# A hand-written issue order remade: batches 1 and 2 read the state in two places, and unread TensorE products stand in four groups instead of three

## The chip, the cores and the metric

The kernel runs on one core of a Trainium2 chip. The metric is the device time of one execution in microseconds (us), lower is better. Five engines work side by side, each through its own instructions in program order: PE (TensorE, the matrix engine; its loads of the stationary operand are shown apart as PEld), DVE (VectorE), ACT (ScalarE), POOL (GpSimd) and SP, which here only starts transfers (DMA) between the main memory and the core. An engine waits for another through semaphores. Matrix products land in PSUM, which holds eight banks of 128 x 512 words here, and have to be copied or used from there by DVE or ACT before the bank is free again.

## The reference

Eight batches, eight heads, 512 tokens and 32 state rows per head, width 64. Tokens attend to the state rows, the state rows attend to the tokens, and both results, side by side along the token axis (512 + 32 = 544 rows of 512 channels for each batch), run through a block with a causal convolution as gate.

```python
scores = x @ state.T / 8;   xread = softmax(scores) @ state     # 512 tokens read the state
scores2 = state @ x.T / 8;  sread = softmax(scores2) @ x        # 32 state rows read the tokens
h = concat([xread, sread])                                      # (8, 544, 512), heads side by side
gate = sigmoid(causal_conv(h, conv_w, 5 taps))
out = (gate * (h @ w_val)) @ w_out
```

(The reference's setup draws 576 rows for the second block's own example; here the block gets the 544 rows above.)

## The kernel before, in words

Every batch b goes through the same steps. `scores` (tile `sc`, two PSUM banks) multiplies the state by the batch's transposed tokens. For the tokens' side DVE transposes the scores in 32 x 32 blocks (`sl`), takes the maximum (`mx`), POOL subtracts and later scales, ACT takes the exponent (`ex`). For the state's side DVE takes the row maximum (`nb`), ACT the exponent (`e2`), PE transposes it (`exp_T`, tile `e2p`), ACT copies it out (`e2T`), and `state_read` multiplies it by the tokens: 32 products of 32 x 64 for a batch, each of two passes, so 64 matrix instructions and 64 weight loads on tile `srp`. `state_read_copy` (tile `sr`), `state_read_T` (tile `srT`) and `state_read_out` turn the result into the 32 extra rows, which a tail treats for all batches at the end. `state_val` (tile `sgv`) multiplies the state by the weights, and `read` (tile `xr`) the probabilities by the state; DVE, ACT and POOL form the convolution gate from `xr` (tiles `acc`, `last`, `sig`). `values` (tile `val`) makes the values, `gated` (tile `g`) multiplies them by the gate, `high` and `low` split `g` into a high part on ACT (`gh`) and a low part on POOL (`gl`), and `project` multiplies by the output weights with three products for each of four channel blocks (tile `op`, lines 512 to 514). ACT or DVE copies `op` to `o`, and SP stores it. Batch 0 is treated in a simpler form: its `values` products use plain four-byte data and take longer (tile `a0` by `sw0`).

Work of the start: ACT, POOL and DVE decode the weights, which lie in memory as 64-bit words (`words_part`, `words_side`, `words_sum`, `words_join`: tiles `wt`, `ws`, `wv`, `wc`), and PE spreads the convolution weights over partitions (tile `cwbp`, copied by ACT to `cwb`; tile `cwtp`, copied to `cwt`). POOL multiplies the state by `cwb` for batch 0 (`tap_state`, shown as z<-z,cwb).

`warm_up` multiplies a tile of ones by itself, `n` products of 128 x 128 in two passes each. Nothing reads the result. `WARM` gives the size of each group.

What runs when is written out by hand. All steps are numbered in the order in which the batches' code lists them; `ORDER` is a list of these numbers, and the last loop of the kernel issues them in that order, with a letter where the engine can be chosen (a is ACT, v or none is DVE, g is POOL). Each engine therefore gets its instructions in the order of this list. `SLOTS` says for each new tile which of its buffers it takes; `ps` is the list of PSUM banks.

Of the kernel before, what the change touches and what calls it, by code (L numbers as in the profile page):

```python
# [36 lines left out]
WARM = (9, 2, 14)  # L37
# [3 lines left out]
68 15 0 8 69 20 25 158 2 6 1 55 40 9 969 71 10a 35 11 74 73 12 75 970 72 30 81 13 76g 14a 82 22a 91 70 77 83 21 78 84g  # L41
267 26 89 79g 85 23 27a 86 971 18 16 92 28 3 87g 96 19a 24 17a 160 90 29 109g 80 97a 103 88 94 105a 57g 104a 171 110
95a 169 172 161 56 162 37a 58 170 163 32g 36 31 59 176 42a 38 45 122 164g 114 93 4 33 115 39 41 118 34 116 66g 177a 43
165 123 67g 106 44 117 269 166 124a 50 111g 108a 185 7 125g 107a 159 47a 271 98 60a 167g 99 119 46 178 268 280 100 126
376 48 281 594 61g 270 120a 49 52a 130 121g 272 62a 51 127 63g 188a 140 53 179a 287 128a 131 273g 134 186a 54 141 5
278 64a 146 168 288a 65g 147 279 187 135 274 129g 189 190 132a 275 133g 101 191 136 173a 148 193 276g 142 194 102a
199a 237 195 198 149 192a 200 137 196g 201 143 277 152 174g 197 153 284 205 202 154 144a 175 150a 155 207 138a 203g
219 208 156a 139 225 213a 209 151 226 282g 212 157 220 227 206a 214 238 204 221 215 285 228 294 210g 222 229a 216 378
223a 297a 217g 180 485 295a 380 181 145 286a 387 290 224g 182 389 289 388 298 183 239 184a 230g 218 379 231 291 232
240 390 299 283g 296 241a 381 211 292 233 293a 394 307 234 334 300 242g 309 328 395a 346 302 321 335 382g 310 329 301a  # L50
340 311 341 303 308a 347 336 323 383 312g 342 304 348 235a 324 243 305g 313 255 325 315a 384 330 236g 322a 256 314 244
326g 306 337 257 316 258 385g 331 245 393 332a 317 246 259a 318 333g 260 403 247a 386 377 338a 248 487 404a 339g 486
406a 396 703 489 327 249 319g 391a 498 250 405 499 251 392g 488 397a 252 349 320 407 261 253a 496 408 490 505 424a 343
# [28 lines left out]
    x="0100101000",  # L82
    xT="01001001",
    sT="01",
    e2="0001000111020202",
    e2T="0120122102101001",
    sr="00000000",
    sl="00101010",
    ah="01001100101",
    al="0110011010",  # L90
    swh="0100110010",
    swl="011001101",
    acc="0120201221022011210102101202",
    last="0110100101011010011110110101",
# [703 lines left out]
```

## Time and profile before

| | |
|---|---|
| median of three runs | 211.48 us (211.03 to 211.58) |
| the profiled execution, its own time | 212.08 us |
| its span, first to last instruction | 209.9 us |
| PE busy | 203.2 us (97%) |
| DVE, ACT, POOL busy | 159.4, 155.2, 152.5 us |

The time of an execution holds some two microseconds that lie around the span. Busy time of PE is the time in which at least one product is shown as running; products overlap, so the distance from one start to the next tells more than the length of one.

### The profile page before, as it was taken

Reading aid. Unit: us, or ns where it says so; the run is one execution under the profiler, and the core shown is the slowest. Engines: PE = TensorE matmul, PEld = TensorE weight load, DVE = VectorE, ACT = ScalarE, POOL = GpSimd, SP = SyncE. Lnnn points to the kernel's source line nnn. Section 1 sums busy time; section 2 is a strip of 40 time slices with the busy share of each in tenths; the row PEclk is TensorE's granted clock in tenths of the full one; section 3 lists DMA queues with packets and bytes.
Section 4 is the critical chain, followed back from the end, with each engine's and each line's share of the span. In section 5 each row is a group of like instructions: output and inputs, shape, how many; then the busy total and the mean of one; then the engine's idle time right before and its main releaser. Section 6 shows DMA issues by size and latency. Waiting matters only on the chain.

```text
span 209.9 us, 4603 instructions
## 1 busy us (share of the span) xinstructions
PE 203.2 (97%) x1781; PEld 147.0 (70%) x1781; DVE 159.4 (76%) x255; ACT 155.2 (74%) x325; POOL 152.5 (73%) x118
## 2 busy tenths in 40 slices
PE   7799999999999999999999999999999999999994
PEld 6654457676688567766777857577866788988883
DVE  1799999998999988998969759998895988630000
ACT  3498999977987978789755989799879964333123
POOL 2286999999979938988938596948799999473000
PEclk9999999999999999999999999999999999999998
DMA  6999689604700692048016028182011200002525
GB/s 182 417 370 425 263 248 425 284 0 153 253 0 2 187 415 100 0 101 303 0 55 250 3 62 279 25 286 103 0 52 53 101 0 3 0 0 100 186 79 188
DMA packets 9507, 31.24 MB, mean 149 GB/s; under 512 B 1146, under 2 KB 1678, under 8 KB 7566
## 3 DMA queue, kind: packets, MB, share of 16 engines
q1 hardware_dynamic: 9342, 30.43, 39.9%
q10 hardware_dynamic: 144, 0.52, 1.0%
q8 instruction: 14, 0.23, 0.4%
q14 instruction: 7, 0.06, 0.1%
HBM read 22.04 MB, written 8.91 MB: 147 GB/s over the span
## 4 chain that ended last, share of the span: by engine, by line
PE 86%; DVE 4%; issue 1%; ACT 1%; ACTq 0%
PE val L503 21%; PE op L512 13%; PE op L514 13%; PE op L513 13%; PE srp L377 4%; PE e2p L368 4%; PE xr L439 3%; PE sgv L324 3%; PE tval L580 3%; PE sc L353 3%; DVE acc L483 2%; PE xr L454 2%; PE top L513 1%; PE top L514 1%; PE top L512 1%
## 5 line engine op out<-in xcount | busy, mean ns | idle before, releaser
L483 DVE SCALAR_TENSOR_TENSOR acc<-xr,cwt,acc 128x511 f32<-128x511 f32 (+2 forms) x84 | 60.3, 741 | 6.0 <-ACT last L216 2.4
L512 PE MATMUL op<-woh,gh 128*128 128x512 f32 x124 | 50.1, 404 | 0.2 <-DVE acc L483 0.2
L514 PE MATMUL op<-woh,gl 128*128 128x512 f32 x124 | 49.1, 396 | 0.0
L513 PE MATMUL op<-wol,gh 128*128 128x512 f32 x124 | 48.9, 394 | 0.0
L221 POOL TENSOR_TENSOR gl<-g,gh 128x512 fp32r<-128x512 f32 x32 | 41.2, 1295 | 7.7 <-ACT gh L208 7.5
L221 POOL TENSOR_TENSOR acc<-acc,last 128x508 f32<-128x508 f32 x28 | 35.9, 1286 | 12.8 <-DVE acc L483 7.0
L512 PEld LDWEIGHTS op<-woh,gh 128*128 128x128 f32 x124 | 23.4, 189 | 6.3 <-issue 0.6
L514 PEld LDWEIGHTS op<-woh,gl 128*128 128x128 f32 x124 | 23.3, 188 | 5.6 <-POOL gl L221 0.3
L513 PEld LDWEIGHTS op<-wol,gh 128*128 128x128 f32 x124 | 23.3, 188 | 5.0 <-issue 0.2
L208 ACT CAST gh<-g 128x512 fp32r<-128x512 f32 x30 | 18.7, 632 | 10.1 <-DVE g L508 8.0
L208 ACT COPY o<-op 128x512 f32<-128x512 f32 (+1 forms) x33 | 18.4, 579 | 10.1 <-PE op L514 8.3
L508 DVE SCALAR_TENSOR_TENSOR g<-sig,val 128x512 f32<-128x512 f32 x32 | 21.3, 675 | 5.7 <-POOL tgl L221 1.5
L216 ACT ACTIVATE last<-xr,cwt 128x508 f32<-128x508 f32 x28 | 19.7, 708 | 6.5 <-DVE acc L483 5.0
L221 POOL TENSOR_TENSOR sl<-sl,mx 128x1024 f32<-128x1024 f32 (+1 forms) x9 | 15.6, 1729 | 7.3 <-DVE mx L410 7.2
L495 ACT ACTIVATE sig<-acc 128x512 f32<-128x512 f32 x28 | 17.9, 641 | 2.6 <-POOL acc L221 2.6
L478 ACT ACTIVATE acc<-xr,cwt 128x512 f32<-128x512 f32 x28 | 19.3, 708 | 0.7 <-PE xr L439 0.5
L221 POOL TENSOR_TENSOR al<-sl,ah 128x1024 fp32r<-128x1024 f32 x7 | 16.9, 2413 | 2.5 <-ACT ah L208 2.3
L503 PE MATMUL val<-ah,swh 128*128 128x512 f32 x56 | 17.2, 403 | 0.0
L503 PE MATMUL val<-al,swh 128*128 128x512 f32 x56 | 17.1, 395 | 0.0
L503 PE MATMUL val<-ah,swl 128*128 128x512 f32 x56 | 16.7, 397 | 0.4 <-issue 0.4
L221 POOL TENSOR_TENSOR ex<-ex,rc 128x1024 f32<-128x1024 f32 (+1 forms) x9 | 15.6, 1729 | 1.6 <-DMA z<-z_in 0.9
L332 DVE SCALAR_TENSOR_TENSOR swl<-sgv,swh 128x512 fp32r<-128x512 f32 x14 | 9.3, 676 | 5.5 <-ACT swh L216 5.5
(120 smaller groups left out, 378.3 us busy)
## 6 DMA issues: line engine op xcount, KB each, us to landing
x<-x_in SPq DMA_DIRECT2D x8, 1024.0 KB, 7.2
out<-o SPq DMA_DIRECT2D x31, 256.0 KB, 2.3
xT<-xT_in SPq DMA_DIRECT2D x7, 1024.0 KB, 10.9
vw<-w_val SPq DMA_DIRECT2D x4, 511.8 KB, 9.4
ow<-w_out SPq DMA_DIRECT2D x4, 511.8 KB, 5.2
xT<-xT_in ACTq DMA_DIRECT2D x1, 512.0 KB, 4.8
xT<-xT_in SPq DMA_DIRECT2D x1, 512.0 KB, 5.3
z<-z_in SPq DMA_DIRECT2D x2, 256.0 KB, 7.9
```

The lines of the kernel that those rows point to most:

```text
L208: nc.scalar.copy(out, in_)
L216: nc.scalar.mul(out, in_, factor)
L221: (nc.vector if e == "DVE" else nc.gpsimd).tensor_tensor(out, a, b, op=how)
L332: nc.vector.scalar_tensor_tensor(get("swl", b)[:, g], get("sgv", b, g), HALF / SCALE, get("swh", b)[:, g].bitcast(F32), op0=ALU.mult, op1= ...
L478: nc.scalar.mul(get("acc", b, pr), pt, cw[:, HALO, pr:pr + 1])
L483: nc.vector.scalar_tensor_tensor(acc[:, d:], get("xr", b, pr)[:, :S - d], cw[:, HALO - d, pr:pr + 1], acc[:, d:], op0=ALU.mult, op1=ALU.add)
L495: nc.scalar.activation(get("sig", b, pr), get("acc", b, pr), AF.Tanh, scale=0.5)
L503: nc.tensor.matmul(get("val", b, k), w[:, g, c], a[:, g], start=(term == 0 and g == 0), stop=(term == terms - 1 and g == NG - 1))
L508: nc.vector.scalar_tensor_tensor(get("g", b, k), get("sig", b, k), 1.0, get("val", b, k), op0=ALU.add, op1=ALU.mult)
L512: nc.tensor.matmul(pt, gh, woh[:, k], start=(k == 0), stop=False)
L513: nc.tensor.matmul(pt, gh, wol[:, k], start=False, stop=False)
L514: nc.tensor.matmul(pt, gl, woh[:, k], start=False, stop=(k == NPR - 1))
```

## The change

The list `ORDER` is replaced by another that holds the same steps, `SLOTS` is replaced by buffers to fit it, and `WARM` has two more entries: 9 + 2 + 7 + 7 + 1 = 26 unread products instead of 9 + 2 + 14 = 25. No function is touched.

```diff
-WARM = (9, 2, 14)
+WARM = (9, 2, 7, 7, 1)
 ORDER = """
-68 15 0 8 69 20 25 158 2 6 1 55 40 9 969 71 10a 35 11 74 73 12 75 970 72 30 81 13 76g 14a 82 22a 91 70 77 83 21 78 84g
+68 15 0 8 69 20 25 2 6 158 1 55 35 10a 969 71 9 40 11 73 74 12 75 970 72 30 82 76g 81 21 91 70 22a 83 971 13 16 77 89
...
 SLOTS = dict(
     ps=
-    "06126005634267501024315671027614305672465276124300127146753231763245041567746302041372520631672135460573642014"
+    "71207370465727576101234607561262571304137153657124001765726513404671053023431637547601543142670635104561075342"
...
```

What the lists do to each engine's instructions is seen in the built programs. Rows read: line, operation, tile written, tiles read, size, and a count of equal neighbours. The number after the tile's name is the batch.

First PE at about a quarter of the program, where batches 1 and 2 read the state. Before:

```order
L353 MATMUL sc_3_1_732<-xT_3_490,sT_0_97 32x512
L377 MATMUL srp_1_745<-x_1_430,e2T_1_0_374 32x64 x16
L377 MATMUL srp_1_745<-x_1_430,e2T_1_1_525 32x64 x16
L377 MATMUL srp_2_788<-x_2_480,e2T_2_1_555 32x64 x16
L377 MATMUL srp_2_788<-x_2_480,e2T_2_0_784 32x64 x16
L393 MATMUL srT_1_831<-ident_64,sr_1_807 128x128
L503 MATMUL val_1_3_614<-ah_1_600,swl_1_563 128x512 x2
L503 MATMUL val_1_2_841<-ah_1_600,swh_1_518 128x512 x2
```

With the change, the same batches:

```order
L503 MATMUL val_1_0_677<-ah_1_619,swl_1_565 128x512 x2
L377 MATMUL srp_1_700<-x_1_480,e2T_1_0_385 32x64 x16
L377 MATMUL srp_1_700<-x_1_480,e2T_1_1_498 32x64 x16
L324 MATMUL sgv_2_0_737<-wv_65,sT_0_97 32x512
```

```order
L393 MATMUL srT_1_770<-ident_64,sr_1_749 128x128
L503 MATMUL val_1_2_772<-ah_1_619,swh_1_521 128x512 x2
L503 MATMUL val_1_3_780<-ah_1_619,swh_1_521 128x512 x2
L503 MATMUL val_1_2_772<-al_1_626,swh_1_521 128x512 x2
L503 MATMUL val_1_2_772<-ah_1_619,swl_1_565 128x512 x2
L503 MATMUL val_1_3_780<-al_1_626,swh_1_521 128x512 x2
L503 MATMUL val_1_3_780<-ah_1_619,swl_1_565 128x512 x2
L377 MATMUL srp_2_810<-x_2_473,e2T_2_0_752 32x64 x16
L377 MATMUL srp_2_810<-x_2_473,e2T_2_1_553 32x64 x16
L439 MATMUL xr_2_0_853<-sl_2_495,z_73 64x512
```

The two reads stood back to back, 64 products or 128 matrix instructions in a row; now `sgv` and `sc` of the next batches, a transpose and twelve `val` products of 512 columns stand between them.

Then PE in the first part, where the unread products stand. Before:

```order
L353 MATMUL sc_0_1_129<-xT_0_94,sT_0_97 32x256
L271 MATMUL cwtp_162<-ident_64,cv_68 128x20
L314 MATMUL warm_2_194<-blank_78 128x128 x14
L261 MATMUL cwbp_1_209<-cv_68,sel_71 128x128
L261 MATMUL cwbp_0_211<-cv_68,sel_71 128x128 x4
L368 MATMUL e2p_0_1_221<-ident_64,e2_0_1_216 128x128 x4
L353 MATMUL sc_1_0_229<-xT_1_106,sT_0_97 32x512
```

With the change:

```order
L353 MATMUL sc_0_1_129<-xT_0_94,sT_0_97 32x256
L314 MATMUL warm_2_173<-blank_78 128x128 x7
L271 MATMUL cwtp_181<-ident_64,cv_68 128x20
L261 MATMUL cwbp_0_183<-cv_68,sel_71 128x128 x4
L261 MATMUL cwbp_1_196<-cv_68,sel_71 128x128
L314 MATMUL warm_3_214<-blank_78 128x128 x7
L368 MATMUL e2p_0_1_222<-ident_64,e2_0_1_209 128x128 x4
L314 MATMUL warm_4_231<-blank_78 128x128
L353 MATMUL sc_1_0_233<-xT_1_108,sT_0_97 32x512
```

The group of 14 is now two groups of 7 on either side of the convolution's products, and one more unread product stands behind the first transposes.

Last ACT at about an eighth of the program, where batch 0's second half of `sgv` is copied out as `sw0`. Before:

```order
L208 COPY e2T_1_0_374<-e2p_1_0_340 128x512
L417 ACTIVATE ex_75<-sl_1_320 128x32x32
L474 ACTIVATE sig_0_3_393<-xr_0_3_277 128x512
L208 CAST gh_0_1_409<-g_0_1_378 128x512
L216 ACTIVATE sw0_0_264<-sgv_0_1_1_383 128x256
L216 ACTIVATE sw0_0_264<-sgv_0_0_1_381 128x256
L287 ACTIVATE ws_o_1_432<-ow1_1_348,edge_70 128x512
L208 CAST woh_66<-wc_o_0_391 128x512
```

With the change:

```order
L417 ACTIVATE ex_75<-sl_1_323 128x32x32
L208 COPY e2T_1_0_385<-e2p_1_0_352 128x512
L208 CAST gh_0_1_423<-g_0_1_380 128x512
L279 ACTIVATE wt_o_1_437<-ow1_1_348,edge_70 128x512
L208 CAST gh_0_0_445<-g_0_0_404 128x512
L287 ACTIVATE ws_o_1_461<-ow1_1_348,edge_70 128x512
L216 ACTIVATE sw0_0_267<-sgv_0_0_1_449 128x256
L216 ACTIVATE sw0_0_267<-sgv_0_1_1_451 128x256
L208 CAST woh_66<-wc_o_0_425 128x512
```

The two copies now stand behind both decoding passes of a weight block and behind `gh` of batch 0, block 0. By `SLOTS` the next transposes of batch 1 (`e2p_1_1`) take the bank of `sgv_0_0_1`, and the next `val` products the bank of `sgv_0_1_1`, so both wait for these copies.

## Rows read from the trace of the kernel before

**Rows 1.** The page: busy time, share of the span, instructions; a DMA queue.

```profile
PE 203.2 (97%) x1781; PEld 147.0 (70%) x1781; DVE 159.4 (76%) x255; ACT 155.2 (74%) x325; POOL 152.5 (73%) x118
...
q8 instruction: 14, 0.23, 0.4%
```

**Rows 2.** Busy by stretch: stretch, length, PE, PEld, DVE, ACT, POOL, clock, DMA, GB/s.

```profile
30.00:40.00 10.00, 10.00 (x53) 6.17 (x52) 9.70 (x14) 9.75 (x20) 10.00 (x9) 1.00 0.95 394
```

**Rows 3.** PE in time at state_read of batches 1 and 2: start, length, instruction, count.

```profile
51.72 2.01 PE L377 MATMUL srp<-x,e2T 128*32 128x64 f32 x128
53.66 0.33 PE L393 MATMUL srT<-ident,sr 128*128 128x128 f32 x1
54.35 0.62 PE L503 MATMUL val<-ah,swl 128*128 128x512 f32 x2 [0.36 <-issue]
54.81 0.63 PE L503 MATMUL val<-ah,swh 128*128 128x512 f32 x2
```

**Rows 4.** PE in time, the same transpose for another batch.

```profile
92.52 0.33 PE L393 MATMUL srT<-ident,sr 128*128 128x128 f32 x1
...
93.16 0.62 PE L503 MATMUL val<-al,swh 128*128 128x512 f32 x2
```

**Rows 5.** DMA queues from 51.5 to 53.1 us: packets, MB, share.

```profile
q8 instruction: 1, 0.02, 5.6%
```

**Rows 6.** The chain that ended last, in order of time: start, us, what.

```profile
23.25 1.98 PE val L503 x4
...
27.54 1.03 PE srp L377 x64
28.57 0.59 PE e2p L368 x4
29.16 3.44 PE val L503 x8
...
33.43 0.44 PE e2p L368 x4
...
51.79 1.94 PE srp L377 x128
```

**Rows 7.** The start in time, three engines.

```profile
13.49 0.66 PE L368 MATMUL e2p<-ident,e 128*128 128x128 f32 x4 [0.41 <-ACT e L361]
13.76 1.27 DVE L304 SCALAR_TENSOR_TENSOR wv<-vw,wt_v 128x512 int32<-128x512 int32 x2
14.55 1.60 POOL L221 TENSOR_TENSOR z<-z,cwb 128x640 f32<-128x640 f32 x1
15.09 0.67 PE L340 MATMUL sgv<-wv,sT 64*32 64x256 f32 x16
16.40 4.54 PE L454 MATMUL xr<-a,z 32*64 32x512 f32 x80
```

**Rows 8.** An unread group of 14 products in time.

```profile
8.39 3.39 PE L314 MATMUL warm<-blank 128*128 128x128 f32 x28
```

**Rows 9.** PE in time at another place where it waits.

```profile
103.57 0.40 PE L514 MATMUL op<-woh,gl 128*128 128x512 f32 x1
104.14 0.47 PE L512 MATMUL op<-woh,gh 128*128 128x512 f32 x1 [0.17 <-DVE acc L483]
```

**Rows 10.** ACT in time around the copies sw.

```profile
25.66 0.59 ACT L474 ACTIVATE sig<-xr 128x512 f32<-128x512 f32 x1
26.13 0.62 ACT L208 CAST gh<-g 128x512 fp32r<-128x512 f32 x1
26.64 0.66 ACT L216 ACTIVATE sw<-sgv 128x256 f32<-128x256 f32 x2
27.18 0.80 ACT L287 ACTIVATE ws_o<-ow,edge 128x512 f32<-128x512 int16 x1
...
28.37 0.76 ACT L279 ACTIVATE wt_o<-ow,edge 128x512 f32<-128x512 int16 x1
```

**Rows 11.** The issue at 2.9 us: KB, us to landing.

```profile
xT<-xT_in SPq DMA_DIRECT2D x1, 1024.0 KB, 9.0
```

More of the change, by code (lines that the diff above doesn't have):

```diff
@@ L40 @@
 ORDER = """
-68 15 0 8 69 20 25 158 2 6 1 55 40 9 969 71 10a 35 11 74 73 12 75 970 72 30 81 13 76g 14a 82 22a 91 70 77 83 21 78 84g
[L42 to L50, printed above, removed]
@@ new lines @@
+207 148 173a 194 137 195 174g 153 138a 200 192a 154 201 143 202 155 196g 175 199a 149 208 144a 285 203g 284 197 277
+225 145 213a 219 226 150a 209 220 212 227 204 221 206a 228 180 282a 214 210g 181 294 222 182 286a 215 378 229a 216
+297a 183 231 387 223a 217g 237 184a 380 295a 232 389 233 224g 218 379 238 156a 239 296 388 230g 157 289 240 211 151
+290 381 7 390 299 283g 4 291 139 234 292 594 300 334 298 394 293a 235a 393 346 302 307 382g 335 340 303 241a 347 309
+301a 341 236g 321 342 310 336 395a 304 348 383 242g 311 328 329 308a 384 330 305g 243 244 312g 323 306 245 315a 331
@@ new lines @@
+621 556a 483a 557g 626 622a 624a 623 616 568g 634 625 617 724a 636 721 704 627 667 569g 478 637 641 655 466 629 656
+618 254 635a 657 484 630 588 722a 631 710 668 638 589 628a 643 619 661 933a 632g 662 644 931a 663 620a 711 669 639g
+649a 576 633 590 720 640 712g 658 577 648 664 591 642a 650 725 645 592a 726 651 646g 814 727 813 652 659a 593 730 825
+653g 823 728 731a 570 815 665a 660g 578 732 654 571 733a 713 647 572 824 816 573 729a 718a 734 579 817 826 735 719g
+580a 670 830 736 581 673 574a 738 674 757 770 575 818g 739 743 675 759 771 737a 832 745 831a 772 666g 819 740 582 746
@@ L76 @@
+875 939 867a 808 883a 788 851 884g 942 948 941 949 864g 943 871g 876 953 950 877a 865 878g 893 952 944 951 872 794
+945a 954 800 946g 795 955a 789 894 956g 796 801 888 909 895g 802 790 809 896g 889a 797 810a 890g 963 811 791 964 792a
+798a 803 793 965 804a 921 805 966 910 967a 922 968 957 903 958 923 959 924 960 915 961a 897 925a 904 926 898 799 962
+899 905 900 906 901a 911 902 907a 912 916 908 913a 917 914 918 919a 920
 """.split()
@@ L89 @@
     ah="01001100101",
-    al="0110011010",
+    al="0111100101",
     swh="0100110010",
     swl="011001101",
-    acc="0120201221022011210102101202",
-    last="0110100101011010011110110101",
-    sig="00123323332233223333223332323322303",
-    g="0101100110101001111010100101010101",
-    gh="0011201100232231045210364126403514620153640",
-    gl="01023121120345203164024361034261305241",
-    o="0123030312111312320301003123020130",
+    acc="0120102112011200102020120120",
+    last="0101010101010110011010101001",
+    sig="00123030333333030333003300303330312",
+    g="0101100101010101011010101001101010",
+    gh="0111032320010013245612305610253142635410625",
+    gl="01230404402315320432512034150243516203",
+    o="0121021023322330010012222013230012",
     nb="00000000",
-    r2="00100000",
+    r2="00111111",
     mx="00000000",
```

55 lines of the change are left out of this document (25 added, 30 removed).

## The prediction

> **What bounds the kernel now.** I read the page first: PE is busy for 203.2 of 209.9 us, DVE, ACT and POOL for a good three quarters [rows 1]. A busy share says little of a pipelined engine, so I went on to PE in time. From 16.40 us to the end one product starts as the one before it has streamed in: two products of 512 columns take 0.46 us, 0.23 each, and only a few starts are later than that [rows 3, 9]. The chain that ended last runs through PE for nearly all of its length, and its pieces give the price of each kind of step in its surroundings [rows 6]. So the time is the sum of PE's products plus what PE waits, and a new order can change three things: waits of PE that go, waits that come, and the small costs of passing from one kind of product to another. The other engines matter through their deadlines. In the stretch from 30 to 40 us DVE, ACT and POOL are busy for 9.70 to 10.00 of 10 us [rows 2], so there a deadline has little slack.
>
> **The wait that the change is about.** The reader is to see one place. After 128 small instructions of `srp` comes the transpose `srT`, and then a `val` product starts 0.69 us later, with 0.36 us idle that no semaphore explains: "issue" [rows 3]. From `srT` to the second pair of `val` products it is 54.81 - 53.66 = 1.15 us, and at another batch, where nothing waits, 93.16 - 92.52 = 0.64 us [rows 4]. The wait costs **0.51 us**. What is it? Queue q8 moved 14 packets in all, 0.23 MB, so 16.4 KB each [rows 1]. PE has 1781 products and 1781 weight loads, 3562 instructions: one packet for 254 of them. So I take q8 for PE's instructions, fetched in blocks. One such packet moves while the 128 products run, which with their loads are 256 instructions in 1.94 us [rows 5, 6], a whole block. Everywhere else in the rows a block's worth holds some products of 512 columns: with only twelve of them in it, it lasts 2.8 us longer. I read the wait as the next block not yet being usable when the last of this one was issued. Against it speaks that the packet was moved by 53.1 us and the wait only starts at 54.0.
>
> Here a page differs. The Trainium skill, "Runtime: NRT & Kernel Launch", section "Instruction fetch mechanics", gives the block as 256 instructions of 16 KiB, with which the packets of q8 agree, but holds the crossing of a block to be "mostly hidden" and PE's store to be 2048 instructions deep. By that rule the 0.36 us would be no fetch, and the change would win nothing here; that is a rival below.
>
> **The change part by part.**
>
> *State reads apart.* Between the two reads there are now `sgv`, `sc`, a transpose and 12 products of 512 columns. The smallest number of microseconds that 256 consecutive instructions take in the new order is then about 1 + 2 + 2.8, some 6 us by the same prices, against 1.94. The 0.51 us go: **-0.51**. The bounds are 0 (it is no fetch) and -0.51. Splitting costs something: a read of 64 passes by itself takes 1.03, the double one 1.94 [rows 6], so 2 x 1.03 - 1.94 = **+0.12**.
>
> *Transposes elsewhere.* `e2p` of batch 2 now stands between batch 0's plain four-byte `val` products. Transposes before such products show 0.59, those between the faster kind 0.44 [rows 6]: **+0.15**. Other transposes change neighbours between cases that cost the same.
>
> *Unread products.* One product more, two passes: 28 passes take 3.39 us, 0.12 each [rows 8], so 0 to +0.24. The two groups of 7 fill time in which PE waits for ACT's exponent anyway (0.41 idle ahead of 13.49 [rows 7]). The single one stands after the transposes, ahead of `sc` of batch 1, where PE runs in one piece to 16.40. But there is slack behind it: `sgv` at 15.09 starts 0.06 after DVE ended the weights it needs (13.76 + 1.27 = 15.03), and `xr` at 16.40 follows POOL's product, which ends at 16.15 [rows 7]; DVE's and POOL's work up to there is the same in number and length. PE may come up to 0.2 us later to both without `xr` starting much later. I take **0**, with +0.24 as the bound. If DVE or POOL were earlier, the cover would be gone and the product would cost its 0.24.
>
> The clock stands at 1.00 of full speed in the stretch shown [rows 2], the 2.4 GHz level, and an unread pass took 0.12 us at 8.39 [rows 8]; with 7 products ahead of the convolution's and 7 behind, PE is as busy as before up to 13 us, so I expect no fall to the 1.2 GHz level.
>
> *Transfers.* SP's order changes too: the rest of `sT` and the first half of `z`, 448 KB, now go ahead of batch 1's tokens, which landed 9.0 us after their issue at 2.9 [rows 11]. At some 400 GB/s [rows 2] they land 1.1 us later, near 13.1, and their first reader is `sc` behind the transposes of 13.49 [rows 7]: no cost, but it becomes one if they slip by another microsecond. Batch 4's tokens go ahead of a weight block that ACT decodes around 31 us; 1 MB at that rate takes 2.6 us, of which about 1 should be over before that block can be issued; so I estimate that it lands up to 1.5 us later than before, inside what ACT has queued ahead of it: 0, bound +0.5.
>
> *The sw copies on ACT.* They now stand behind two more decoding passes and one more cast, 0.76 + 0.80 + 0.62 = 2.18 us, less a `sig` of 0.59 that moved ahead: 1.6 us later, so the first ends near 26.64 + 0.38 + 1.6 = 28.6 [rows 10]. Their reader-to-be, the transposes of batch 1 in the bank that they free, is due on PE at about 28.5 [rows 6]. A wait of about 0.1 to 0.3 us appears. Another of about the same size goes: batch 0's second four `val` passes took 1.98 us where eight took 3.44, 1.72 per four, so 0.26 was waited at 23.25 [rows 6]. I set these against each other: 0.
>
> *Waits further on.* The largest other one is at 104.14, where PE waits for a DVE tap: 0.57 from start to start instead of 0.23, so 0.34 [rows 9]. Banks are handed out anew, so this one can vanish and others can come. The new order's own waits can't be read from this trace. I take as many as before: 0, bounds -0.6 (these two gone and nothing in their place) and +1.2 (twice that added).
>
> **Sum.** -0.51 + 0.12 + 0.15 = -0.24 us. The profiled execution took 212.08 us, 0.3% above the median of 211.48; 0.24 is 0.11% of it. On the median that gives **211.2 us**.
>
> **Rivals.**
>
> *The other waits go as well.* For it: PE waits between 20 and 105 us on single instructions of ACT and DVE, and the new list has other banks and other neighbours there. Against it: the same three engines are as full as before. -0.24 and -0.6, and a few of the small ones, another -0.4: 210.2 us.
>
> *ACT becomes the bound from 26 to 36 us (the other side).* All of the first output products need ACT's casts, POOL's low parts and the banks that ACT frees, with 9.75 of 10 us of ACT taken [rows 2]. If batch 0's block 0 of `g` is late on DVE, its cast `gh` is, and with it the decoding pass and both copies behind it, and PE stands at the transposes of batch 1. For each decoding pass (0.80) and cast (0.62) that slips behind, PE waits that much: 1.4 us, so 211.2 + 1.4 = 212.6. It decides once the copies end more than about 1 us after PE is ready, near 29.5 us. Against it: my sum above has them end within 0.3 of PE.
>
> *The wait was no fetch and stays, or turns up after the next small group.* Then only the costs are left: 211.48 + 0.12 + 0.15 = 211.75 us. For it: the packet that had moved 0.9 us before. The page named above speaks for it too. Against it: the wait stands exactly where a block's worth of small instructions ends, no semaphore explains it, and no other group of 64 has one [rows 6].
>
> **How the numbers follow.** My forecast 0.48, the waits gone 0.24, ACT the bound 0.16, no fetch 0.12. The forecast's own range is 210.7 to 211.8. The range for 8 in 10 reaches to the two outer cases, 210.0 to 212.5. About 0.3%, 0.63 us, is what a measurement here can tell from no change: under 210.85 lies the second case and some 0.08 of the first, over 212.11 the third and 0.02 of the first. Faster 0.32, same 0.50, slower 0.18.
>
> **What would show it.** The two `srp` groups with 64 instructions each and no idle "issue" behind either: right. An idle of 0.3 us or more without a releaser after any small group: the wait was no fetch or the block boundary fell elsewhere. `xr` of batch 0 should start between 16.3 and 16.7 us. The transposes of batch 1 in 27 to 30 us show whether ACT's copies hold PE; output products should begin between 32.5 and 33.3 us. At about 57 us, ahead of the transposes of batch 3, PE should be 0.2 to 0.4 us ahead of before, and what is added or lost after that is the new order's other waits. The prediction is wrong if those sum to more than 0.6 us on either side, or if the clock is below 1.00 anywhere ahead of the tail.

## The result, and the profile after

The changed kernel is slower: a median of 212.80 us against 211.42 us, a ratio of 1.0068 with a 95% interval of 1.0054 to 1.0082. That is 1.4 us more, where the forecast was 0.3 us less, and it lies outside the range of 210.0 to 212.5 us. One of the six executions took 216.45 us, at a mean granted clock of 0.992; the ratio leaves it out. The profiled execution took 212.77 us with a span of 210.9 us.

The page: busy time, share of the span, instructions; and the queue that the prediction took for PE's program [rows 1].

```profile
PE 205.8 (98%) x1783; PEld 148.2 (70%) x1783; DVE 158.6 (75%) x255; ACT 154.3 (73%) x324; POOL 152.9 (72%) x119
...
q8 instruction: 14, 0.23, 0.5%
```

PE is busy for 2.6 us more with two instructions more. The busy times of the other three engines move by less than 1 us, with one instruction fewer on ACT and one more on POOL. So PE waits inside its products' shown time. First the place that the change is about, PE in time after the change (start, length, instruction, count), to be held against [rows 3].

```profile
48.63 1.10 PE L377 MATMUL srp<-x,e2T 128*32 128x64 f32 x64
49.66 1.09 PE L324 MATMUL sgv<-wv,sT 64*32 64x512 f32 x16
50.54 1.06 PE L353 MATMUL sc<-xT,sT 64*32 64x512 f32 x16
51.54 0.33 PE L393 MATMUL srT<-ident,sr 128*128 128x128 f32 x1
51.62 1.17 PE L503 MATMUL val<-ah,swh 128*128 128x512 f32 x4
...
54.57 1.10 PE L377 MATMUL srp<-x,e2T 128*32 128x64 f32 x64
55.60 1.14 PE L439 MATMUL xr<-sl,z 32*64 32x512 f32 x16
```

Each read has its 64 instructions, `val` follows `srT` by 0.08 us, and no idle "issue" is left. The change did here what it says, and not by the luck of one execution: in all six profiles of the new order (this one and five runs below) the step from `srT` to `val` is 0.08 to 0.09 us. Now the place where the time went, batch 7's scores. PE and ACT in time after the change:

```profile
133.66 1.10 PE L377 MATMUL srp<-x,e2T 128*32 128x64 f32 x64
...
134.69 1.70 PE L353 MATMUL sc<-xT,sT 64*32 64x512 f32 x9
...
135.10 0.59 ACT L208 COPY o<-op 128x512 f32<-128x512 f32 x1 [1.50 <-DMA out<-o]
135.58 0.53 ACT L390 ACTIVATE sr<-srp,r 128x64 f32<-128x64 f32 x2
...
135.73 0.18 PEld L353 LDWEIGHTS sc<-xT,sT 64*32 64x32 f32 x14 [0.91 <-ACT o L208]
...
137.61 0.33 PE L393 MATMUL srT<-ident,sr 128*128 128x128 f32 x1
```

And the same in the trace of before:

```profile
134.62 1.09 PE L353 MATMUL sc<-xT,sT 64*32 64x512 f32 x16
135.50 1.06 PE L324 MATMUL sgv<-wv,sT 64*32 64x512 f32 x16
136.50 0.33 PE L393 MATMUL srT<-ident,sr 128*128 128x128 f32 x1
```

From the start of `sc` to `srT` it is 1.88 us before and 2.92 us after. The rows tell why, read backwards: the second half of `sc` loads its weights when ACT's copy of an output tile ends, because `SLOTS` gives it that tile's PSUM bank (2). ACT's copy begins 1.50 us late, because it waits for a store from the output buffer (0) that it wants to fill. SP's issues after the change (tile, engine, count, KB, us from issue to landing), in two short stretches at 124.55 and 126.83 us:

```profile
x<-x_in SPq DMA_DIRECT2D x1, 1024.0 KB, 6.6
...
out<-o SPq DMA_DIRECT2D x1, 256.0 KB, 8.2
```

The store stands in SP's line behind a load of 1 MB and three other stores and lands at 135.02 us. Two banks were idle all the while: 0 since 132.63 us and 1 since 133.23 us, by the last use of each tile. `SLOTS` gives them to later tiles.

The rest is found by cutting PE's program at places where both orders have done the same number of products. All in us; the three further profiles of before are runs told of below.

| stretch | before, as shown | before, three more | after |
|---|---|---|---|
| start of `xr` of batch 0 | 16.40 | 15.98, 15.98, 15.95 | 16.33 |
| from there to `xr` of batch 1 | 20.88 | 20.94, 20.85, 20.89 | 20.76 |
| to `xr` of batch 3 (the two reads lie here) | 37.88 | 37.41, 37.78, 37.69 | 37.60 |
| to `sgv` of batch 5 | 46.20 | 46.21, 46.21, 46.26 | 46.65 |
| to `xr` of batch 6 | 19.92 | 19.90, 19.90, 19.91 | 20.72 |
| to `srT` of batch 7 | 18.51 | 18.52, 18.50, 18.53 | 18.57 |
| to the end of the span | 50.11 | 50.14, 50.18, 50.07 | 50.28 |
| time outside the span | 2.18 | 2.15, 2.14, 2.17 | 1.87 |

From `xr` of batch 0 to that of batch 3 the kernel got shorter, by 0.41 us against the execution shown and by 0.17 us against the mean of the three others. Everything behind it got longer, by 1.44 us in all against the same mean. The first `xr` begins 0.36 us later in the span than in the three others, and the time outside the span is 0.28 us less. Where that lies is not shown for certain: in all ten profiles of the old order, altered or not, a transfer of 8 KB on queue q14 ends 2.0 to 2.2 us behind the last instruction, and in the six of the new order there is none, so it seems to lie behind the span.

The stretch with the two reads shows what the change is worth there. Two further profiles of the old order (the kernel with seven unread products fewer and the one with two pairs of banks exchanged, both below) have no stall behind the reads, and in both it is 37.36 us. Against that the execution shown is 0.52 us longer and the three others 0.05, 0.42 and 0.33. In the six profiles of the new order it is 37.55 to 37.60 us. So the stall is gone, and the new order pays about 0.2 us for it.

### The profile page after: what moved, and what is told of

Its sections match the earlier page's. It is cut to its first block, busy times and chain, and to the rows that moved or that the text cites. A ratio compares the mean times of both kernels' runs of the same rounds, so it can differ in the third digit from the quotient of the medians.

```text
span 210.9 us, 4598 instructions
## 1 busy us (share of the span) xinstructions
PE 205.8 (98%) x1783; PEld 148.2 (70%) x1783; DVE 158.6 (75%) x255; ACT 154.3 (73%) x324; POOL 152.9 (72%) x119
## 4 chain that ended last, share of the span: by engine, by line
PE 82%; ACT 6%; DVE 4%; POOL 3%; DMA 2%; issue 1%; SPq 0%; DVEq 0%; ACTq 0%
PE val L503 20%; PE op L512 13%; PE op L514 13%; PE op L513 13%; PE xr L439 4%; PE srp L377 3%; PE sc L353 3%; PE sgv L324 3%; PE tval L580 3%; PE e2p L368 2%; DMA cww<-conv_w 2%; POOL ws_v L289 1%; ACT acc L478 1%; ACT gh L208 1%; POOL ws_o L289 1%
## 5 line engine op out<-in xcount | busy, mean ns | idle before, releaser
L483 DVE SCALAR_TENSOR_TENSOR acc<-xr,cwt,acc 128x511 f32<-128x511 f32 (+2 forms) x84 | 59.4, 739 | 4.8 <-ACT xt L479 3.6
L208 ACT COPY o<-op 128x512 f32<-128x512 f32 (+1 forms) x33 | 18.9, 580 | 17.4 <-PE op L514 12.0
L208 ACT CAST gh<-g 128x512 fp32r<-128x512 f32 x28 | 17.4, 625 | 6.1 <-PE op L513 3.9
L503 PE MATMUL val<-ah,swh 128*128 128x512 f32 x56 | 18.1, 415 | 0.1
```

The source lines that it names most:

```text
L208: nc.scalar.copy(out, in_)
L483: nc.vector.scalar_tensor_tensor(acc[:, d:], get("xr", b, pr)[:, :S - d], cw[:, HALO - d, pr:pr + 1], acc[:, d:], op0=ALU.mult, op1=ALU.add)
L503: nc.tensor.matmul(get("val", b, k), w[:, g, c], a[:, g], start=(term == 0 and g == 0), stop=(term == terms - 1 and g == NG - 1))
```

## The experiments

The theory after this reading: the change's own gain is there but small, and the loss is in the buffers that the new `SLOTS` hands out, above all one store in SP's line. The rivals: PSUM banks are simply short in the new order, whatever is copied when; or each wait that is taken away comes back at the next one. And two questions on the gain: is the stall behind the reads a matter of where the reads stand against a block of PE's program, and how large is it in an ordinary execution?

### The stores: three ways to take the wait away

One digit of an output buffer:

```diff
-    o="0121021023322330010012222013230012",
+    o="0121021023322330310012222013230012",
```

> Changed kernel, with one digit of SLOTS altered: tile o of batch 4, block 3 takes output buffer 3, whose store landed at about 133.1 us, instead of buffer 0, whose store landed at 135.02 us. Theory (the loss is mostly one chain: ACT waits 1.50 us for a store that lies behind a load of 1 MB in SP's queue, so the PSUM bank it copies from comes free 1.05 us late for sc of batch 7): ACT's wait is under 0.1 us, sc and sgv at 134.7 us take 1.88 us instead of 2.92 us, and the time falls by 0.7 to 1.05 us, to 211.75 to 212.1 us. Rival (PSUM banks are short there whatever ACT does): another bank or another copy keeps PE, 212.6 to 212.8 us.

Measured: 211.76 us, 1.04 less than the changed kernel; 1.0025 of before, 1.0012 to 1.0038. (The medians of the altered kernels come from other comparisons than the changed kernel's, with medians of before from 211.14 to 211.47 us. By the ratios, each taken within its own comparison, the gain here is 0.9 us.) Its PE and ACT in time:

```profile
134.16 0.59 ACT L208 COPY o<-op 128x512 f32<-128x512 f32 x1 [0.15 <-PE op L514]
135.09 1.09 PE L353 MATMUL sc<-xT,sT 64*32 64x512 f32 x16
...
135.97 1.06 PE L324 MATMUL sgv<-wv,sT 64*32 64x512 f32 x16
...
136.97 0.33 PE L393 MATMUL srT<-ident,sr 128*128 128x128 f32 x1
```

ACT now waits for PE's product and no store, and from `sc` to `srT` it is 1.88 us, as before; the stretch from `sgv` of batch 5 to `xr` of batch 6 falls from 20.72 to 19.69 us. The theory holds with its full price, and the first rival falls here: no other bank was in the way.

The bank alone, with ACT still waiting (banks 0 and 2 exchanged in `SLOTS` from the second half of `sc` of batch 7 to the end):

```diff
-    "54133163702365031742560251537231401473250621651256730426263715267043743250724",
+    "54133163702365031742560251537031421473052601651056732406063715067243743052704",
```

> Changed kernel, with PSUM banks 0 and 2 exchanged from the second half of sc of batch 7 on, so that this tile takes bank 0, free since 132.63 us, and not bank 2, which ACT's late copy frees at 135.68 us; the output buffers stay as they are. Theory (the bank passes on the wait of ACT's copy, and the same ACT also copies sr, which frees the bank of the next sgv): sc no longer waits, but sgv waits for sr's copy until about 136.15 us where 135.6 us would do; half of the 1.05 us is gained, 212.3 us. Rival (the choice of the bank is the whole cause): all of it, 211.75 us. Rival (no wait of this place counts, since DVE sets the later work): 212.8 us.

Measured: 212.33 us, 0.47 less; 1.0056 of before, 1.0042 to 1.0070, an interval that overlaps the changed kernel's, so the time alone does not show the gain. Its PE and ACT in time:

```profile
134.47 1.09 PE L353 MATMUL sc<-xT,sT 64*32 64x512 f32 x16
134.81 0.59 ACT L208 COPY o<-op 128x512 f32<-128x512 f32 x1 [1.44 <-DMA out<-o]
...
135.87 1.09 PE L324 MATMUL sgv<-wv,sT 64*32 64x512 f32 x16 [0.32 <-ACT sr L390]
136.90 0.33 PE L393 MATMUL srT<-ident,sr 128*128 128x128 f32 x1
```

`sc` runs through, and PE meets ACT's lateness one step later, at the bank that the copy of `sr` frees. From `sc` to `srT` it is 2.43 us, 0.49 less than in the changed kernel. In the trace that is half of the price, as expected: the store makes ACT late, the bank decides when PE feels it.

The place in SP's line alone (484 is the store, 704 the load of `x` of batch 6):

```diff
-621 556a 483a 557g 626 622a 624a 623 616 568g 634 625 617 724a 636 721 704 627 667 569g 478 637 641 655 466 629 656
-618 254 635a 657 484 630 588 722a 631 710 668 638 589 628a 643 619 661 933a 632g 662 644 931a 663 620a 711 669 639g
+621 556a 483a 557g 626 622a 624a 623 616 568g 634 625 617 724a 636 721 484 704 627 667 569g 478 637 641 655 466 629 656
+618 254 635a 657 630 588 722a 631 710 668 638 589 628a 643 619 661 933a 632g 662 644 931a 663 620a 711 669 639g
```

> Changed kernel with one transfer moved in SP's line and nothing else: the store of batch 3, block 3 is issued ahead of the 1 MB load of x of batch 6 (its copy was done at about 122.65 us, the load starts at 124.55 us), where it stood behind it and three other stores and landed at 135.02 us. The output buffers and PSUM banks are those of the changed kernel. Theory (ACT's wait of 1.50 us is for a place in SP's line, not for a lack of buffers): the store lands near 125 us, ACT's wait goes, sc and sgv of batch 7 take 1.9 us instead of 2.92 us, and the time is that of the kernel with the other output buffer, 211.76 us. Rival (the copy is late for another reason, or the load of x comes late now and keeps the state read of batch 6): 212.6 us or more.

Measured: 212.03 us; 1.0040 of before, 1.0026 to 1.0054. The store's row in that run:

```profile
out<-o SPq DMA_DIRECT2D x1, 256.0 KB, 2.1
```

It takes 2.1 us instead of 8.2, ACT's wait at 134 us is gone, and from `sc` to `srT` PE takes 1.88 us. So buffers were not lacking; the store was late. The time fell by 0.77 us by the medians, less than with the other buffer, though the two intervals overlap. The profiled execution is the slowest of the five (212.39 us), and it shows one way in which something can come back; whether the others had it is not known:

```profile
101.09 0.58 ACT L208 COPY o<-op 128x512 f32<-128x512 f32 x1 [0.40 <-DMA out<-o]
101.72 0.50 PE L512 MATMUL op<-woh,gh 128*128 128x512 f32 x1 [0.61 <-ACT o L208]
```

That is a store of batch 2 behind two loads of 1 MB, which landed at 101.06 us here and at 100.2 us in the changed kernel's profile, 0.13 us ahead of the same copy.

### The other new waits

The changed kernel's second and third largest new waits are at 79.97 us, where `val` starts 0.48 us after the product ahead of it, and at 101.06 us, where `op` starts 0.39 us after the last transpose does. In both another bank had been free for over 1.5 us. On top of the output buffer of the first kernel above, banks 1 and 2 are exchanged from `val` of batch 3, block 0 on, and then 1 and 5 from `op` of batch 3, block 1 on:

```diff
-    "71207370465727576101234607561262571304137153657124001765726513404671053023431637547601543142670635104561075342"
-    "54133163702365031742560251537231401473250621651256730426263715267043743250724",
+    "71207370465727576101234607561262571304137153657124001765726513404671053023431637547601543241670635204562075345"
+    "14233263705361032745160512137532402473510652612516730456563721567043743510754",
```

> Changed kernel with its three largest new waits taken away by the choice of buffers alone: output buffer 3 for o of batch 4, block 3; banks 1 and 2 exchanged from val of batch 3, block 0 on (80.0 us); and then banks 1 and 5 exchanged from op of batch 3, block 1 on (101.1 us), so that each of these tiles takes a bank that has long been free. The order of instructions stays. Theory (what the changed kernel lost it lost by these buffers): 1.04 us for the first, as measured, 0.25 and 0.36 us for the banks: 212.80 - 1.65 = 211.15 us, level with before. Rival (the next wait for DVE, ACT or POOL takes the gain of the two banks back): as with the first alone, 211.76 us.

Measured: 211.52 us; 1.0012 of before, 1.0003 to 1.0020. By the medians the two banks gave 0.24 us on top of the output buffer and not 0.61; the two intervals overlap, so that size is not certain. PE in time in that run:

```profile
102.37 0.40 PE L514 MATMUL op<-woh,gl 128*128 128x512 f32 x1
102.82 0.73 PE L503 MATMUL val<-ah,swh 128*128 128x512 f32 x2
...
103.87 0.39 PE L514 MATMUL op<-woh,gl 128*128 128x512 f32 x1
104.26 0.73 PE L503 MATMUL val<-ah,swh 128*128 128x512 f32 x2
```

0.45 and 0.39 us from start to start instead of 0.23: 0.22 and 0.16 us of what was saved are waited here, for banks that ACT's copies free. At these two places the second rival is right for the larger part, as far as this profile shows.

A fourth buffer, that of the copy at 100.4 us:

```diff
-    o="0121021023322330310012222013230012",
+    o="0121021023022330310012222013230012",
```

> Changed kernel with the three alterations of buffers of the earlier run and a fourth: o of batch 2, block 0 (about 100.4 us) takes output buffer 0 instead of 3, whose store lies behind two loads of 1 MB in SP's line and landed at 100.2 to 101.1 us, just as ACT came to the copy. Theory (this is the same mechanism at a second place, and it sets when ACT goes on there): ACT's copy starts earlier and no longer with the landing, PE's waits at 102.8 and 104.3 us (0.22 and 0.16 us) shrink, 211.2 to 211.35 us. Rival (ACT is just busy there, the store is not in its way): 211.5 us as with three.

Measured: 211.46 us, level with before (1.0004, 0.9994 to 1.0015). Against the three alterations it is 0.06 us, which is not told from none: nearer to the rival's 211.5 than to the theory's 211.2 to 211.35. Nor is it the forecast's 0.24 us less than before: in its profile all behind `xr` of batch 3 is still 0.30 us longer than in the three further profiles of before. Its ACT in time shows the next store in line:

```profile
107.96 0.58 ACT L208 COPY o<-op 128x512 f32<-128x512 f32 x1 [0.71 <-DMA out<-o]
```

### The stall behind the reads: where and how large

Kernel before, with seven unread products fewer, so that all of PE's later program stands 28 instructions nearer its start:

```diff
-WARM = (9, 2, 14)
+WARM = (9, 2, 7)
```

> Kernel before, with the third group of unread products cut from 14 to 7 and nothing else: 7 products of two passes are 14 weight loads and 14 matrix instructions fewer, so everything behind stands 28 instructions nearer the start of PE's program. The two state reads stay back to back, 128 matrix instructions and as many loads in a row. Theory (the stall behind them was a fetch of a block of PE's program that had begun just as the run began): the block ends 28 instructions later in the program, that is behind srT and some long val products, the transfer that took 1.43 us is down by then, and the step from srT to val falls from 687 ns to under 100; about 0.5 us less, 210.9 us. Rival (the run itself is too dense, wherever blocks end): the step stays near 690 ns, 211.4 us. Second rival (seven products fewer let the clock fall before the convolution's products): the first xr begins 0.1 to 0.5 us later and eats the gain.

Its PE in time:

```profile
53.40 0.33 PE L393 MATMUL srT<-ident,sr 128*128 128x128 f32 x1
53.48 0.71 PE L503 MATMUL val<-ah,swl 128*128 128x512 f32 x2
```

The reads are still back to back, and the stall is gone from this execution. That alone does not show that the shift did it, since an unshifted program (the one with banks exchanged, below) has an execution without the stall too; both show that the density of the run alone doesn't make it. But the time did not fall. The median was 212.38 us (1.0045 of before, 1.0020 to 1.0070): the second rival came true, in part of the executions. Four had a mean granted clock of 1.00 and took 211.02 to 211.37 us; seven had one of 0.98 to 0.99 and took 212.27 to 214.28 us. And the four are hardly faster than before (median 211.31 in that comparison). That was the first sign that the 0.51 us are not there in every execution. The profile says more: its first `xr` begins 0.29 us later than in the three further profiles of before, and the stretch with the reads is 37.36 us, 0.05 to 0.42 less than theirs. So the gain is there in this execution, and part of it was lost at the start.

Kernel before, unaltered, for more profiles:

> Kernel before, unaltered, for a second profile of it. The profiled execution of before took 212.08 us and stands above all other 25 times of this kernel (210.94 to 211.86, median 211.31); the cut of the unread products took the stall behind the state reads away and its undisturbed executions are at 211.02 to 211.37, no faster. Theory (the stall is no fixed cost: it was there in that one execution, whose transfer of a program block took 1.43 us where the others of its kind took 0.9 to 1.0): an execution of about 211.3 us shows srT to val in 85 to 100 ns. Rival (the stall is there each time, and the 0.7 us are elsewhere, as in a later start): the same step takes near 690 ns again.

> Kernel before once more, as the run ahead of it, for a third profile. Same two expectations: 85 to 100 ns from srT to val in an execution of about 211.3 us if the stall comes and goes; near 690 ns if it is always there.

> Kernel before once more, for another pair of transfer and stall. Theory (the block can be used some 1.3 to 1.4 us after its transfer ends, and PE stalls if it gets there earlier): with a transfer of 0.9 to 1.0 us that begins as the reads begin, srT to val takes 85 to 225 ns; with one of 1.25 us or more, 450 ns or more. Rival (the two are not tied): any other pairing.

They took 211.25, 211.54 and 211.47 us, with steps of 0.22, 0.61 and 0.51 us. For the first two 85 to 100 ns or near 690 ns were expected: the first lies between, the second nearer to the rival's. The third had a transfer (below) between the two sizes that its expectation named. So the stall differs from one execution to the next, but is not simply there or gone. PE in time in the first:

```profile
53.30 0.33 PE L393 MATMUL srT<-ident,sr 128*128 128x128 f32 x1
53.52 0.63 PE L503 MATMUL val<-ah,swl 128*128 128x512 f32 x2
```

in the second,

```profile
53.21 0.33 PE L393 MATMUL srT<-ident,sr 128*128 128x128 f32 x1
53.82 0.62 PE L503 MATMUL val<-ah,swl 128*128 128x512 f32 x2 [0.28 <-issue]
```

and in the third:

```profile
53.23 0.33 PE L393 MATMUL srT<-ident,sr 128*128 128x128 f32 x1
53.74 0.62 PE L503 MATMUL val<-ah,swl 128*128 128x512 f32 x2 [0.18 <-issue]
```

The queue's row of the DMA view from 51 to 53 us (its packets, MB, share of 16 engines' time in these 2 us) in the first,

```profile
q8 instruction: 1, 0.02, 3.0%
```

the second

```profile
q8 instruction: 1, 0.02, 4.4%
```

and the third:

```profile
q8 instruction: 1, 0.02, 3.5%
```

A share of 3.0% is 0.03 x 16 x 2 = 0.96 us of transfer, 4.4% is 1.41, 3.5% is 1.12 (1.11 in the packet's record). The execution shown first has 5.6% of 1.6 us, 1.43 us [rows 5]. The kernel with two pairs of banks exchanged (below; same order of PE) has 3.0% of 2 us, and PE in time:

```profile
53.35 0.33 PE L393 MATMUL srT<-ident,sr 128*128 128x128 f32 x1
53.44 0.71 PE L503 MATMUL val<-ah,swl 128*128 128x512 f32 x2
```

So there are five pairs:

| transfer, us | from `srT` to `val`, us |
|---|---|
| 0.96 (banks exchanged) | 0.09 |
| 0.96 | 0.22 |
| 1.11 | 0.51 |
| 1.41 | 0.61 |
| 1.43 | 0.69 |

The longer the transfer, the longer the stall. In the four that stall, `val` starts 1.28 to 1.40 us after the transfer's end in the packet records. As far as five pairs show, the stall is what is left of a transfer and a fixed time behind it, and it goes from nothing to 0.6 us from one execution to the next. The one profile that the forecast was made from had the longest, and its first `xr` began 0.4 us later than in the other three.

Separating the reads in kernel before, the direct test of the change's idea, took three tries. First four `val` products between the reads, with `srT` of batch 1 left behind the second:

```diff
-223a 297a 217g 180 485 295a 380 181 145 286a 387 290 224g 182 389 289 388 298 183 239 184a 230g 218 379 231 291 232
+223a 297a 217g 180 485 295a 380 181 145 286a 387 239 231 290 224g 182 389 289 388 298 183 184a 230g 218 379 291 232
-    "06126005634267501024315671027614305672465276124300127146753231763245041567746302041372520631672135460573642014"
+    "06126005634267501024315671027614305672465276124300127146753123763245041567746302041372520631672135460573642014"
```

> Kernel before, with four val products of batch 1 (two of tile val_1_3, two of val_1_2) moved from behind the two state reads to between them, and the PSUM banks listed in the new order of allocation; all else as before. Theory (the fetch is worth half a microsecond wherever it is taken away, and nothing behind it takes the gain back): no idle time behind srT, 0.5 us less than before, 210.9 us. Rival (the gain is given back at the next wait for DVE or ACT): PE is ahead at 57 us, but at 104 or 137 us it waits by as much more, 211.4 us.

Measured: 212.45 us (1.0055, 1.0043 to 1.0067). No stall behind `srT`, but from `xr` to the next `srT` it took 1.93 us instead of 1.05: the last bank of `xr` waited for the copy of the second read, and ACT had been held up by the later `srT`. Neither expectation: the edit made a wait of its own. Then `srT` of batch 1 ahead of the second read, and banks 2 and 5 exchanged from the last `xr` of batch 2 on (only the order is shown). Against the try before:

```diff
-223a 297a 217g 180 485 295a 380 181 145 286a 387 239 231 290 224g 182 389 289 388 298 183 184a 230g 218 379 291 232
+223a 297a 217g 180 485 295a 380 181 145 286a 387 239 231 224g 182 389 388 298 183 290 184a 230g 218 289 379 291 232
```

> Kernel before with the two state reads apart, done so that no new wait is made of it: between them stand four val products of batch 1 and the transpose srT of batch 1, which keeps its early place so that ACT is not held up, and the last xr of batch 2 takes bank 5, which is free since 53.5 us, instead of that of the second read. Theory (separating the reads takes away a stall that an ordinary execution does not have): no change beyond the two extra group ends of 0.1 to 0.2 us: 211.2 to 211.5 us. Rival (the stall is in every execution): 0.5 us less, 210.8 us.

Measured: 212.26 us (1.0042, 1.0028 to 1.0055). PE in time:

```profile
55.18 1.87 PE L439 MATMUL xr<-sl,z 32*64 32x512 f32 x16
56.98 0.33 PE L393 MATMUL srT<-ident,sr 128*128 128x128 f32 x1
```

1.80 us, 0.75 too much again, since the bank chosen is still read by ACT's exponent: neither expectation once more. With the banks as they were, but for the order of allocation (`srp_1`, `val_1_2`, `srT_1`, `srp_2` in banks 3, 1, 3, 2), and the same order of issue:

```diff
-    "06126005634267501024315671027614305672465276124300127146753231763245041567746302041372520631672135460573642014"
+    "06126005634267501024315671027614305672465276124300127146753132763245041567746302041372520631672135460573642014"
```

> Kernel before with the two state reads apart as in the second try (four val products of batch 1 and srT of batch 1 between them), but with the last xr of batch 2 left in the bank of the second read, which ACT's copy of sr frees in time; in the second try it had taken a bank that ACT's exponent still read until 55.9 us, and xr took 1286 ns instead of 527. Theory (the stall behind the reads is what is left over of a program block's transfer: 0.14 us where that takes 0.96 us, about 0.5 us where it takes 1.4 us, which is rare; and two more group ends cost 0.14 us): no measurable change, 211.1 to 211.4 us. Rival (an ordinary execution has half a microsecond of stall): 210.8 to 210.9 us.

Measured: 211.60 us against 211.36 (1.0009, 1.0001 to 1.0018). All eleven times lie between 211.48 and 211.75, those of before between 211.00 and 212.07. From `xr` of batch 0 to `srT` of batch 7 it takes 143.06 us, where four profiles of before take 142.98 to 143.39; its first `xr` starts at 16.33 us, 0.36 later than in the three further ones. Separating the reads alone gains nothing that can be measured: the time is just above the 211.1 to 211.4 us expected, and the stretch with the reads takes 37.83 us, as long as in an execution of before with a stall, so this way of separating costs what it saves. The late start does not come from the split: with banks exchanged as well (below) the first `xr` starts at 16.02 us. In all ten profiles of the old order the first `xr` follows the second half of batch 0's scores by 8.76 or 8.77 us, and that half starts at 7.57 us here, at 7.62 in the execution shown first and at 7.18 to 7.21 in the three others: it differs from one execution to the next.

Kernel before with two pairs of banks exchanged,

```diff
-    "06126005634267501024315671027614305672465276124300127146753231763245041567746302041372520631672135460573642014"
-    "375631520132715604234721237631500675123420124710253601714572056031437240534",
+    "06126005634267501024315671207614325670465076104322107146753031763045241567746320241370502631670135462573640214"
+    "735671502170315624074301073671522635107402104312057621314530256271473042574",
```

> Kernel before, order untouched, two pairs of PSUM banks exchanged: from wt of the output weights' block 0 on banks 0 and 2 (val of batch 0, block 0 then takes a bank free since 22.31 us, not one freed at 22.79 us, with PE ready at 22.65 us), and from op of batch 3, block 1 on banks 3 and 7 (free since 101.67 us, not 103.17 us, with PE ready at 102.97 us). Theory (waits of PE for a bank that another free bank would spare are pure loss): 0.2 and 0.35 us, 210.75 us. Rival (they come back at the next wait, as 0.37 of the 0.61 us did in the changed kernel): 211.1 to 211.3 us.

and the same exchanges in the clean split:

> Kernel before with both: the two state reads apart as in the clean split, and the two pairs of banks exchanged. Theory (the stall is small in an ordinary execution): as with the banks alone, 210.7 to 210.8 us, with fewer executions above it. Rival (the stall is half a microsecond): 210.3 us.

Measured: 211.17 us (0.9991, 0.9981 to 1.0002) and 211.41 us (0.9999, 0.9990 to 1.0009). The banks alone are the fastest version here, but the interval takes in 1: not shown to beat before, and what the rival expected (211.1 to 211.3). With the split it is neither expectation, 0.6 us above the theory's: its stretch with the reads takes 37.80 us, where that of the banks alone takes 37.36. The wait at 104 us [rows 9] is gone in the trace of the banks alone, and the stretch from `xr` of batch 0 to `srT` of batch 7 takes 142.61 us, with no stall in that one execution.

## Why the prediction was wrong, step by step

**State reads apart, -0.51.** The place and the mechanism hold, as far as they were tested: no semaphore, the stall is in none of the six profiles with the new order, and in the old one it grows with the block's transfer. That the block's place decides rests on one profile, with seven unread products fewer. The size does not hold. It was taken from one execution, which lies near the top of what this kernel does (95 executions in all comparisons: 210.94 to 212.16 us, median 211.34): 0.51 there, and by the same subtraction 0.05, 0.43 and 0.33 in the three others. The sum was then set on the median as if every execution paid it. That the profiled execution stood 0.6 us above the median was in the table, and it was the hint. The Trainium skill, "Runtime: NRT & Kernel Launch", section "Instruction fetch mechanics", calls a block's crossing "mostly hidden"; in the five profiles it is hidden fully once, and 0.14 to 0.6 us show in the others.

**Splitting, +0.12, and the transposes, +0.15; the single unread product, 0.** From `xr` of batch 0 to that of batch 3 the changed kernel is 0.41 us shorter than the execution shown; the forecast of these terms with the stall is 0.24, and the stated "0.2 to 0.4 us ahead at 57 us" was 0.22. That is against the one execution: against the three others it was 0.33 to 0.62 us behind at 57 us. Splitting cost what was said, 1.03 + 1.03 us for the two reads against 1.94. The transposes of batch 2 take 0.44 us to the next start, where they took 0.35 to 0.41 in the four profiles of before: less than the 0.15 set. `xr` of batch 0 began at 16.33 us, inside 16.3 to 16.7, but the single product was not free. PE, DVE and POOL in time after the change:

```profile
13.27 0.66 PE L368 MATMUL e2p<-ident,e 128*128 128x128 f32 x4 [0.46 <-ACT e L361]
13.41 1.27 DVE L304 SCALAR_TENSOR_TENSOR wv<-vw,wt_v 128x512 int32<-128x512 int32 x2
...
13.77 0.39 PE L314 MATMUL warm<-blank 128*128 128x128 f32 x2
...
14.22 1.59 POOL L221 TENSOR_TENSOR z<-z,cwb 128x640 f32<-128x640 f32 x1
...
14.96 0.76 PE L340 MATMUL sgv<-wv,sT 64*32 64x256 f32 x16
...
16.33 4.54 PE L454 MATMUL xr<-a,z 32*64 32x512 f32 x80
...
32.43 0.79 PE L512 MATMUL op<-woh,gh 128*128 128x512 f32 x1
```

From the first transposes to `xr` it is 3.06 us in all six profiles of the new order and 2.88 to 2.91 in the ten of the old one. The step from the transposes to `sc`, where the product stands, grew by 0.22 us, and 0.15 us are still there at `xr`. The cover that the prediction counted on was gone, as it said it might be: DVE's weights end 0.27 us ahead of `sgv` and not 0.06, and POOL's product 0.52 us ahead of `xr` and not 0.25 [rows 7]. The output products began at 32.43 us, just ahead of the stated 32.5 to 33.3.

**The clock, two groups of 7.** Granted clock 1.00 from 8 to 205 us in the profiled execution after the change: right there.

**The sw copies on ACT.** Forecast: the first ends near 28.6 us and PE waits 0.1 to 0.3 us at about 28.5. After the change, PE and ACT in time:

```profile
28.05 0.63 ACT L216 ACTIVATE sw<-sgv 128x256 f32<-128x256 f32 x2
...
28.46 0.65 PE L368 MATMUL e2p<-ident,e 128*128 128x128 f32 x4 [0.23 <-ACT sw L216]
```

The first ends at 28.41 us. Right, in place and size, and the wait at 23.25 us is gone, as forecast. So the rival that ACT becomes the bound from 26 to 36 us did not happen.

**Transfers, 0, bound +0.5.** Right for the loads of the start: batch 1's tokens landed at 13.14 us (13.1 forecast), ahead of their reader at 14.08, and the weight block landed 0.7 us later than before (29.78 against 29.06), where up to 1.5 was said. What was not looked at is stores: output buffers were never named in the prediction, although the change hands out all of `o` anew.

**Waits further on: as many as before, 0, bounds -0.6 and +1.2.** This is the step that failed: new waits were set at 0 because the old trace could not show them, and the new `SLOTS` and SP's order, which could be read, were not followed. All behind `xr` of batch 3 is 1.44 us longer. The store and the output buffer behind it are 1.04 us of that by the medians (0.9 by the ratios, 1.03 in the trace's stretch), the two banks at 80 and 101 us about 0.24, and the rest, with a fourth buffer, can't be told from nothing: with four buffers or banks chosen otherwise and its order untouched, the new list is level with before. That it is level and not 0.24 us faster fits the sizes above, a stall smaller in most executions than the one priced, and costs of about 0.2 us in the stretch with the reads and 0.15 us around the single product. The price of the largest, 1 us for one wait, is twice the largest wait that the old trace showed, which is why a bound made of doubled old waits was too small. The prediction even held two pieces of it in hand: `SLOTS` was in the diff, and SP's order had been read for loads.

**The rivals.** None of the three came true. The other side happened, by another mechanism: not ACT too full, but ACT held by a store.

## What to carry to other kernels

Where a change hands out buffers anew, follow each output buffer to the store that it was last used for, and that store to its place in the line of its queue: a copy that waits for a store stuck behind a 1 MB load holds up the engine, then the PSUM bank, then PE. A stall that no semaphore explains has to be seen in more than one execution before it is priced; hold the profiled execution's own time against the median first. And a wait for a bank, when another bank has long been free, is taken away by one digit, but look at once at who waits next.

## What the runs showed of the hardware

A 256 KB store landed 2.1 us after its issue when no other transfer was under way, and 8.2 us after it when it was issued behind 1 MB of load and three stores on the same queue. The Trainium skill, "DMA: Bandwidth & Descriptors", section "Two DMAs through the same engine are not ordered", says that within one queue of one DMA engine descriptors start in order. The landings agree: the load and three of the four stores behind it, in the order of their issue, at 131.14, 133.78, 134.40 and 135.02 us (that of the first store is not in the trace).

A transfer of 16.4 KB of PE's program took less than 1.05 us in 152 of the 224 cases in all profiles, 1.15 to 1.81 us in 39, and what makes it longer stays open. Where PE stalled, it did not go on before 1.28 to 1.40 us after such a transfer had ended.

Seven unread products fewer (14 to 7 at 8.3 us, so that PE stood for 1.96 us ahead of the first transposes in the one profile) left the mean granted clock at 0.98 to 0.99 in seven of eleven executions, which were 0.9 us or more longer than the other four; where in those seven the clock fell is not shown.
